# An attention and mixture-of-experts kernel: rows of q and k and gathered rows transposed as f32r instead of f32

## The chip, the cores and the metric

The kernel runs on 1 core of one Trainium2 chip. A core has five engines that run side by side, each with its own queue: PE (TensorE, matrix products into PSUM), DVE (VectorE), ACT (ScalarE), POOL (GpSimd) and SP (SyncE, which here only issues DMAs). PEld is the part of PE that loads the stationary operand. All DMAs of a core share 16 DMA engines. The metric is the device time of one execution in microseconds, lower is better. Before the change three runs took 766.83, 770.14 and 770.59 us (median 770.14).

## What is computed

First an attention with a hash mask: batch 4, 8 heads, 768 positions, head dimension 64. A query sees only keys whose six sign bits (of x times a random projection) agree with its own.

```python
q_bits = (np.einsum('bhsd,dk->bhsk', q, proj) > 0)
k_bits = (np.einsum('bhsd,dk->bhsk', k, proj) > 0)
mask = q_bucket[:, :, :, None] == k_bucket[:, :, None, :]   # buckets are the bits read as a number
scores = np.where(mask, scale * q @ k^T, -1e9)
attn = softmax(scores)
x = (attn @ v) as [3072 tokens, 512]
```

Then one expert of eight for each token, of sizes 512 to 1024 to 512:

```python
logits = x @ w_gate + modality_bias[modality_id]
e_idx = np.argmax(logits, axis=1); gate_w = softmax(logits) at e_idx
out[tokens of e] = gate_w * (relu(x @ w1[e]) @ w2[e])
```

All inputs and outputs are float32.

## The kernel before

**Numbers as two parts.** A float32 matrix product is made of f32r products, a form of float32 that PE takes in one pass: an operand is split into a rounded part and a residue (`m1` and `s2`, `xh` and `xl`, `hi` and `lo`), and two or three products are summed in PSUM. Which form PE uses is set by the type of the tiles.

**Attention.** The work goes by pairs of heads, 16 pairs, numbered i (0 to 15). The loop over i runs `score(i)` (scores and exponentials), `maxp(i + 1)` (the maxima that the softmax subtracts), `turn(i + 2)` and `signs(i + 2)` (rows of q and k transposed, hash bits), `residues(i + 2)` (the rounded parts and residues, and DMAs from SBUF to SBUF that spread them over the other 64 partitions), `weigh` (the product with v) and some pieces of the row sums and the router. The order on PE is written out by hand: `PLAN0` for i = 0, `PLAN` for 1 to 14, `LAST` for 15, one string for each of six steps `kt`, one letter for a piece. `T` is one group of four transposes of `turn` (three groups to a pair) or the hash bits, `R` the residues, `L` the load of pair i + 3, `l` the load of v. The other engines and SP's DMAs are put in order by a scheduler, which follows this order and what is ready; SP works its queue strictly in order.

**Rows of q and k.** `load(i)` (L117) issues four DMAs on SP, one each for q and k of each head of the pair, into a tile `qk` of which there are two (pool `ld`). Each has 768 pieces of 256 bytes, since q and k lie side by side in the tile. `turn(i)` (L288) transposes four blocks of 128x128 into a PSUM tile `psx` (L299), the moving operand being the unit matrix `ident` (f32), and ACT copies the tile back over the same place of `qk` (L300), the "raw rows", which the hash bits (L218) and the residues (L307, L308) read. Pair 1 has a form of its own, `second` (L252), and pair 0 too (L184).

**Experts.** Tokens are gathered by slots of 512 rows: `gather` (L925) fetches rows of x from DRAM by an indirect DMA of POOL into `xg`, `xprep` (L941) transposes them, four 128x128 blocks for each `psx` tile (L956), ACT and DVE split them into `xh` and `xl`, and `gemm1` (L967) and `gemm2` (L1008) multiply. Six slots of 512 rows and one of 128 (L949) are always run.

**Two unit matrices.** `ident` is f32, `identr` its copy in f32r, made by POOL (L159). `identr` is used for the transposes of the maxima (L368), whose input `nm` or `nw` is an f32r tile.

Of the kernel before, what the change touches and what calls it, by code (L numbers as in the profile page):

```python
# [10 lines left out]
F32 = mybir.dt.float32  # L11
# [9 lines left out]
NT = S // 128  # L21
# [15 lines left out]
    "SRMSeMSMx",  # L37
    "SFfEMSfMSMF",
    "fSMSMMEBABSe",
# [5 lines left out]
    "MSMlSMRM",  # L45
    "SMSMML",
    "MMBASB",
# [45 lines left out]
def attention(ctx, actx, tc, a, x_d, l_d, route=None, setup=None, before_last=None):  # L93
# [20 lines left out]

    st, fin = {}, {}

    def load(i, heads=(0, 1), parts=1):  # L117
        b, c = i // 4, i % 4
        t = st.setdefault(i, {})
        if "qk" not in t:  # L120
            t["qk"] = ld.tile([P, 2, NT, 2, D], F32, name="qk")
        n = NT // parts
        for h in heads:
            qk = t["qk"][:, h]
            for lo in range(0, NT, n):
                for x, src in enumerate((q, k)):
                    nc.sync.dma_start(out=qk[:, lo:lo + n, (x + 1 + h) % 2], in_=src[b, 2 * c + h].rearrange("(p t) d -> p t d", t=NT)[:, lo:lo + n])
# [10 lines left out]
    nc.scalar.dma_start(out=zst[64:128, 6:12], in_=proj)  # L138
    load(0, (0,), 2)
    ident = fconst.tile([P, P], F32, name="ident")  # L140
    nc.scalar.dma_start(out=ident, in_=a["c_id"])
# [8 lines left out]
    fold = fconst.tile([P, TT], F32, name="fold")  # L150
    identr = const.tile([P, P], F32R, name="identr")
    masks = [const.tile([P, S], F32, name=f"mask{j}") for j in range(2)]
# [99 lines left out]
    def second():  # L252

        t = st[1]
        t.update(gens[0])
        rows = t["qk"].rearrange("p h t x d -> p (h t x d)")
        raw = t["raw"] = [rows[:, h * S:(h + 1) * S] for h in range(2)]
# [30 lines left out]
    def turn(i):  # L288

        t = st[i]  # L290
        t.update(gens[(i + 2) % 3])
        rows = t["qk"].rearrange("p h t x d -> p (h t x d)")
        raw = t["raw"] = [rows[:, h * S:(h + 1) * S] for h in range(2)]
        todo = [(h, tt) for h in range(2) for tt in range(NT)]
        for g in range(0, len(todo), 4):
            part = todo[g:g + 4]
            tp = ps_x.tile([P, MAIN], F32, name="psx")
            for j, (h, tt) in enumerate(part):
                nc.tensor.transpose(tp[:, j * P:(j + 1) * P], t["qk"][:, h, tt].rearrange("p x d -> p (x d)"), ident)  # L299
            nc.scalar.copy(out=rows[:, g * P:(g + 4) * P], in_=tp)  # L300
            yield
# [278 lines left out]
    with tc.manual_schedule(engines={mybir.EngineType.PE}):  # L580
        load(1)
        load_v(0)
        load(2)
        constants()
        with tc.manual_schedule(engines={mybir.EngineType.DVE, mybir.EngineType.Activation, mybir.EngineType.Pool}):
# [16 lines left out]
        for i in range(NPR):  # L602
# [8 lines left out]
            for kt in range(NT):  # L611
# [5 lines left out]
                for c in (PLAN0 if i == 0 else LAST if i == NPR - 1 else PLAN)[kt]:  # L617
# [20 lines left out]
                    elif c == "L":  # L638
                        if i + 3 < NPR:
                            load(i + 3)  # L640
                    elif c == "l":
                        if i + 1 < NPR:
                            load_v(i + 1)
                    elif c == "F" and i % 4 == 0 or c == "f" and i % 4 == 1:
                        next(fins, None)
                    elif c == "e" and i % 4 >= 2 or c == "E" and i == NPR - 2:
                        next(fins, None)
                    elif c == "x" and i % 4 == 2 or c == "y" and i % 4 == 3:
                        next(xs, None)
                        next(xs, None)  # L650
        for _ in avs:
            pass
    return finish, finish_x, ps_x, ident, fold, marks

# [219 lines left out]

def experts(ctx, tc, a, x_d, tab, out, ps_x, ident, fold, marks):
    nc = tc.nc
    w1, w2 = a["moe_w1"], a["moe_w2"]
    gp = ctx.enter_context(tc.tile_pool(name="gp", bufs=1))
# [46 lines left out]
    def gather(s):  # L925
# [4 lines left out]
        nc.sync.dma_start(out=tb[:, 0:n], in_=tab[bass.ds(o, n * P), :].rearrange("(p a) w -> p a w", a=n))  # L930
        xg = gp.tile([P, TS // P, DM], F32, name="xg", bufs=XG)
        src, at = x_d, tb[:, :, 0:1]
# [4 lines left out]
        for g in range(n):  # L937
            nc.gpsimd.indirect_dma_start(out=xg[:, g], out_offset=None, in_=src, in_offset=bass.IndirectOffsetOnAxis(ap=at[:, g], axis=0))  # L938
        return tb, xg

    def xprep(s, xg, dst):  # L941
# [4 lines left out]
        if nt(s) == 1:  # L946
            tp = ps_x.tile([P, 4, P], F32, name="psx")
            for c in range(4):
                nc.tensor.transpose(tp[:, c], xg[:, 0, c * P:(c + 1) * P], ident)  # L949
            nc.scalar.copy(out=xh[:, :, 0:P], in_=tp)  # L950
            nc.vector.tensor_tensor(out=xl[:, :, 0:P], in0=tp, in1=xh[:, :, 0:P].bitcast(F32), op=ALU.subtract)
            return
        for c in range(4):
            tp = ps_x.tile([P, TS], F32, name="psx")
            for g in range(nt(s)):
                tr = nc.tensor.transpose(tp[:, g * P:(g + 1) * P], xg[:, g, c * P:(c + 1) * P], ident)  # L956
                if s == ("e", 0):
# [227 lines left out]
def body(tc, a, out):  # L1185
# [4 lines left out]
    with ExitStack() as ctx, ExitStack() as actx:  # L1190
        route, early_slots, late_slots, setup = router(ctx, tc, a, x_d, tab)
        finish, finish_x, ps_x, ident, fold, marks = attention(ctx, actx, tc, a, x_d, None, route, setup, lambda sp: eslot.append(early_slots(sp)))
        actx.close()
        runner, tabs, conditional, yp, late_area, tiny = experts(ctx, tc, a, x_d, tab, out, ps_x, ident, fold, marks)
        r = runner()
# [38 lines left out]
```

## Time and profile before

| | |
|---|---|
| runs, us | 766.83, 770.14, 770.59 |
| profiled execution, us | 766.3 |
| its span (first to last instruction), us | 764.4 |
| PE busy | 744.9 us, 97% |
| DVE, ACT, POOL busy | 65%, 48%, 57% |
| DMA of SP's queue | 83.79 MB, 44.4% of the 16 engines |

How to read it: PE is busy nearly all the time, but a matrix product is pipelined, and its "busy" time holds its latency, so that the share alone does not say whether PE could do more. What PE's work costs in time is read from the starts of consecutive instructions. The span has four parts: a start of about two passes, up to 58 us; the attention's steady loop, up to 444 us; the expert slots, up to about 710 us; and an end.

### The profile page before, as it was taken

How to read it: one execution, taken by the hardware profiler on the slowest of the kernel's cores; microseconds unless marked ns; L12 is line 12 of the kernel's file. 1: busy time of each engine (PE TensorE's matmuls, PEld its weight loads, DVE VectorE, ACT ScalarE, POOL GpSimd, SP SyncE). 2: the span in 40 equal slices, each digit the busy share in tenths (PEclk: the TensorE clock that was granted, in tenths of full speed). 3: DMA queues.
4: the chain of work that ended last, by engine and by line, in shares of the span. 5: the costliest groups of instructions: out<-in, count | busy, mean ns of one | idle time of the engine just before them, and what ended most of it. 6: DMA issues, size and time to landing. Idle time of an engine off the chain costs nothing.

```text
span 764.4 us, 12253 instructions
## 1 busy us (share of the span) xinstructions
PE 744.9 (97%) x4308; PEld 527.8 (69%) x4308; DVE 499.3 (65%) x878; ACT 367.2 (48%) x649; POOL 438.6 (57%) x335
## 2 busy tenths in 40 slices
PE   7899999999999999999999999999999999999995
PEld 3566666566656666666666657888888877788884
DVE  6987778788777887976986887844333343334423
ACT  5455565555555556556564563244243432434343
POOL 7697779769878868987869974622222202202011
PEclk9999999999999999999999999999999999999998
DMA  8655454526766435665343154665444754444332
GB/s 191 141 127 126 91 123 114 130 67 120 130 132 140 112 85 125 134 120 141 91 101 60 56 194 129 112 216 179 139 156 134 254 196 138 143 123 137 103 109 74
DMA packets 103528, 99.26 MB, mean 130 GB/s; under 512 B 60333, under 2 KB 80717, under 8 KB 103456
## 3 DMA queue, kind: packets, MB, share of 16 engines
q1 hardware_dynamic: 97312, 83.79, 44.4%
q0 software_dynamic: 4832, 12.94, 4.8%
q10 hardware_dynamic: 1312, 1.65, 1.1%
q8 instruction: 36, 0.59, 0.3%
q14 instruction: 36, 0.29, 0.2%
HBM read 59.33 MB, written 13.14 MB: 95 GB/s over the span
## 4 chain that ended last, share of the span: by engine, by line
PE 83%; issue 9%; DVE 3%; DMA 1%; POOL 1%; ACT 1%; SPq 0%; POOLq 0%; DVEq 0%; ACTq 0%
PE psu L457 16%; PE pss L404 9%; PE pss L405 8%; PE psm L339 6%; PE hps L974 5%; PE hps L975 5%; PE hps L976 5%; PE yps L1017 4%; PE yps L1015 4%; PE yps L1016 4%; PE psm L345 3%; PE psx L299 2%; PE psu L218 2%; PE psx L480 2%; PE psx L542 1%
## 5 line engine op out<-in xcount | busy, mean ns | idle before, releaser
L441 POOL TENSOR_TENSOR sp<-sp,pb 128x768 f32<-128x768 f32 x124 | 225.8, 1855 | 14.1 <-ACT pb L438 13.2
L341 DVE TENSOR_REDUCE mx<-psm 128x1 f32<-128x512 f32 x192 | 130.1, 687 | 26.4 <-PE psm L339 24.1
L424 ACT ACTIVATE pb<-pss 128x512 f32<-128x512 f32 x186 | 111.3, 599 | 60.2 <-PE pss L405 51.6
L457 PE MATMUL psu<-pb,vt 128*64 128x512 f32 (+1 forms) x768 | 134.4, 492 | 0.0
L922 DVE TENSOR_TENSOR w<-raw,w 128x1024 fp32r<-128x1024 f32 x52 | 65.6, 1264 | 100.7 <-ACT w L918 100.2
L457 PEld LDWEIGHTS psu<-pb,vt 128*64 128x64 f32 x768 | 50.9, 136 | 69.9 <-issue 60.0
L918 ACT CAST w<-raw 128x1024 fp32r<-128x1024 f32 x56 | 58.5, 1049 | 79.1 <-PE yps L1017 72.2
L438 ACT ACTIVATE pb<-pss 128x512 f32<-128x512 f32 x93 | 55.6, 598 | 81.2 <-PE pss L405 79.4
L1084 POOL DMA_INDIRECT out<-y,tb x25 | 24.8, 990 | 106.5 <-ACT y L1083 102.9
L441 POOL TENSOR_TENSOR sp<-pb,pb 128x768 f32<-128x768 f32 x31 | 56.2, 1836 | 50.0 <-ACT pb L438 50.0
L1015 PE MATMUL yps<-w,hl 128*128 128x512 f32 x200 | 79.5, 397 | 0.0
L1017 PE MATMUL yps<-w,hh 128*128 128x512 f32 x200 | 78.2, 391 | 0.0
L1016 PE MATMUL yps<-w,hh 128*128 128x512 f32 x200 | 77.9, 389 | 0.0
L974 PE MATMUL hps<-xh,w 128*128 128x512 f32 x192 | 75.4, 394 | 0.0
L938 POOL DMA_INDIRECT xg<-x_d,tb x17 | 18.2, 1069 | 98.8 <-DMA tb<-tab 95.2
L975 PE MATMUL hps<-xl,w 128*128 128x512 f32 x192 | 74.9, 390 | 0.0
L976 PE MATMUL hps<-xh,w 128*128 128x512 f32 x192 | 74.7, 390 | 0.0
L404 PE MATMUL pss<-m_0g,s_0g 128*128 128x512 f32 (+1 forms) x186 | 69.5, 374 | 0.4
L979 ACT ACTIVATE hh<-hps 128x512 fp32r<-128x512 f32 x48 | 28.7, 598 | 83.4 <-PE hps L976 83.4
L980 DVE SCALAR_TENSOR_TENSOR hl<-hps,hh 128x512 fp32r<-128x512 f32 x48 | 33.2, 691 | 53.7 <-ACT hh L979 53.4
L347 DVE TENSOR_REDUCE mx<-psm 128x2 f32<-128x512 f32 x96 | 66.1, 688 | 1.2
L404 PE MATMUL pss<-m_1g,s_1g 128*128 128x512 f32 (+1 forms) x186 | 65.9, 355 | 0.1
(266 smaller groups left out, 1428.4 us busy)
## 6 DMA issues: line engine op xcount, KB each, us to landing
raw<-moe_w SPq DMA_DIRECT2D x56, 512.0 KB
vt<-v SPq DMA_DIRECT2D x16, 384.0 KB
qk<-q SPq DMA_DIRECT2D x31, 192.0 KB
qk<-k SPq DMA_DIRECT2D x31, 192.0 KB
s_0g<-m_0g SPq DMA_DIRECT2D x30, 192.0 KB
s_1g<-m_1g SPq DMA_DIRECT2D x30, 192.0 KB
x_d<-xs SPq DMA_DIRECT2D x18, 256.0 KB
tw<-moe_w SPq DMA_DIRECT2D x2, 2048.0 KB
```

Source lines behind the costliest of these rows:

```text
L341: marks["m"] = nc.vector.tensor_reduce(out=mx[:, qt + j, hi, 0:1], in_=mp, axis=AX.X, op=ALU.max).ins
L347: nc.vector.tensor_reduce(out=mx[:, qt:qt + 2, hi, 1], in_=mp, axis=AX.X, op=ALU.max)
L404: nc.tensor.matmul(out, t["s1"][h][:, ks], t["m1"][h][:, cs], start=True, stop=False)
L424: marks["p"] = nc.scalar.activation(t["pb"][kt][:, h, 0:MAIN], sp, AF.Exp, scale=0.125).ins
L441: marks["add"] = (nc.vector if h and i in CFG["spd"] else nc.gpsimd).tensor_tensor(out=t["sp"][:, h], in0=(t["pb"][0] if kt == 1 else t["s ...
L457: marks["u", kt] = nc.tensor.matmul(t["u"][part][64 * h:64 * h + 64, 0:w], t["v"][:, h, kt], t["pb"][kt][:, h, COLS[part]], start=False, s ...
L974: nc.tensor.matmul(hps, lo[:, c, fs], xh[:, c], start=(c == 0), stop=False)
L975: nc.tensor.matmul(hps, hi[:, c, fs], xl[:, c], start=False, stop=False)
L976: nc.tensor.matmul(hps, hi[:, c, fs], xh[:, c], start=False, stop=(c == 3))
L1015: nc.tensor.matmul(yps[g], hl[fc][:, gs], hi[:, fb], start=(fc == 0), stop=False)
L1016: nc.tensor.matmul(yps[g], hh[fc][:, gs], lo[:, fb], start=False, stop=False)
L1017: nc.tensor.matmul(yps[g], hh[fc][:, gs], hi[:, fb], start=False, stop=(fc == 7))
```

## The change

Pairs 3 to 15 of q and k no longer go to SBUF directly. A new `stage(i)` copies them by four DMAs from DRAM to a scratch tile in DRAM that has the layout of `qk`, and `load(i)` fetches that with one DMA into an f32r tile. `stage(3)` stands after `load(2)` ahead of the loop, and a new letter `c` in step 4 of the plans stages pair i + 4. For these pairs `turn` transposes as f32r with `identr`. The raw rows get a tile of their own: in `turn` the other one of the two `qk` tiles, in `second` one of the two `sp` tiles. The gathered rows `xg` are an f32r tile too, written by the indirect DMA under the name of f32, and transposed as f32r. `identr` moves to another pool, and the experts use it in place of `ident` (as f32 where they need that).

```diff
-    "SFfEMSfMSMF",
+    "ScFfEMSfMSMF",
...
-    "SMSMML",
+    "SMSMMLc",
...
+    scratch = {}
+
+    def stage(i):
+
+        b, c = i // 4, i % 4
+        scratch[i] = tc.dram_tile([P, 2, NT, 2, D], F32, name=f"qk_d{i}")
+        for h in range(2):
+            for x, src in enumerate((q, k)):
+                nc.sync.dma_start(out=scratch[i][:, h, :, (x + 1 + h) % 2], in_=src[b, 2 * c + h].rearrange("(p t) d -> p t d", t=NT))
 
     def load(i, heads=(0, 1), parts=1):
         b, c = i // 4, i % 4
         t = st.setdefault(i, {})
+        if i in scratch:
+            t["qk"] = ld.tile([P, 2, NT, 2, D], F32R, name="qk")
+            nc.sync.dma_start(out=t["qk"].bitcast(F32), in_=scratch[i])
+            return
...
+    identr = fconst.tile([P, P], F32R, name="identr")
     ident = fconst.tile([P, P], F32, name="ident")
...
-    identr = const.tile([P, P], F32R, name="identr")
...
@@ second
-        rows = t["qk"].rearrange("p h t x d -> p (h t x d)")
+        rows = spool.tile([P, 2, S], F32, name="sp").rearrange("p h s -> p (h s)")
...
@@ turn
-        rows = t["qk"].rearrange("p h t x d -> p (h t x d)")
+        rows = ld.tile([P, 2, S], F32, name="qk").rearrange("p h s -> p (h s)")
...
-                nc.tensor.transpose(tp[:, j * P:(j + 1) * P], t["qk"][:, h, tt].rearrange("p x d -> p (x d)"), ident)
+                nc.tensor.transpose((tp.bitcast(F32R) if i in scratch else tp)[:, j * P:(j + 1) * P], t["qk"][:, h, tt].rearrange("p x d -> p (x d)"), identr if i in scratch else ident)
...
         load(2)
+        stage(3)
...
+                    elif c == "c":
+                        if i + 4 < NPR:
+                            stage(i + 4)
...
-        xg = gp.tile([P, TS // P, DM], F32, name="xg", bufs=XG)
+        xg = gp.tile([P, TS // P, DM], F32R, name="xg", bufs=XG)
...
-            nc.gpsimd.indirect_dma_start(out=xg[:, g], out_offset=None, in_=src, in_offset=bass.IndirectOffsetOnAxis(ap=at[:, g], axis=0))
+            nc.gpsimd.indirect_dma_start(out=xg[:, g].bitcast(F32), out_offset=None, in_=src, in_offset=bass.IndirectOffsetOnAxis(ap=at[:, g], axis=0))
...
-                tr = nc.tensor.transpose(tp[:, g * P:(g + 1) * P], xg[:, g, c * P:(c + 1) * P], ident)
+                tr = nc.tensor.transpose(tp.bitcast(F32R)[:, g * P:(g + 1) * P], xg[:, g, c * P:(c + 1) * P], identr)
```

The order of instructions on the engines shows what the scheduler makes of it. First PE in the second pass of the loop, where pair 3 is turned, before (L299 is the transposes, L404 and L405 the scores of pair 1, L339 and L345 the maxima of pair 2):

```order
L339 MATMUL psm<-s_0g_115,m_0g_113 128x512
L404 MATMUL pss<-m_0g_102,s_0g_104 128x512
L405 MATMUL pss<-m_0g_106,s_0g_108 128x512
L299 MATMUL psx<-ident,qk 128x128 x4
L404 MATMUL pss<-m_1g_103,s_1g_105 128x512
L405 MATMUL pss<-m_1g_107,s_1g_109 128x512
L299 MATMUL psx<-ident,qk 128x128 x4
L339 MATMUL psm<-s_0g_115,m_0g_113 128x512
```

And PE at the same place now (the lines have new numbers: L312 is the transposes, L417, L418, L352 are L404, L405, L339 of before):

```order
L352 MATMUL psm<-s_0g_115,m_0g_113 128x512
L417 MATMUL pss<-m_0g_102,s_0g_104 128x512
L418 MATMUL pss<-m_0g_106,s_0g_108 128x512
L312 MATMUL psx<-identr,qk 128x128 x4
L417 MATMUL pss<-m_1g_103,s_1g_105 128x512
L418 MATMUL pss<-m_1g_107,s_1g_109 128x512
L312 MATMUL psx<-identr,qk 128x128 x4
L352 MATMUL psm<-s_0g_115,m_0g_113 128x512
```

Nothing moved on PE; `identr` stands for `ident`, in 39 groups of four.

Next SP at the start, before, from the load of v on (L206 and L207 spread the residues of pair 0, the four L127 load pair 2, the rest are small constants):

```order
L133 DMA vt<-v 128x2x384
L206 DMA m_0g_128<-m_0g_124 64x768
L207 DMA s_0g_130<-s_0g_126 64x768
L588 DMA wg<-moe_w_gate 128x4x8
L706 DMA ktok<-c_tok 128x24
L706 DMA ke_66<-c_e 128x24
L127 DMA qk<-q 128x6x64
L127 DMA qk<-k 128x6x64
L127 DMA qk<-q 128x6x64
L127 DMA qk<-k 128x6x64
L206 DMA m_1g_129<-m_1g_125 64x768
L207 DMA s_1g_131<-s_1g_127 64x768
```

SP at the start now (L124 is the copies to the scratch, L140 the loads, L219 and L220 are L206 and L207 of before):

```order
L146 DMA vt<-v 128x2x384
L124 DMA qk_d_204<-q 128x6x64
L124 DMA qk_d_204<-k 128x6x64
L124 DMA qk_d_204<-q 128x6x64
L124 DMA qk_d_204<-k 128x6x64
L140 DMA qk<-q 128x6x64
L140 DMA qk<-k 128x6x64
L140 DMA qk<-q 128x6x64
L140 DMA qk<-k 128x6x64
L219 DMA m_0g_128<-m_0g_124 64x768
L220 DMA s_0g_130<-s_0g_126 64x768
L219 DMA m_1g_129<-m_1g_125 64x768
```

The copies for pair 3 and the loads of pair 2 moved ahead of the spread of head 0 of pair 0, and the small constants went further back, behind the mask rows of pair 1 (L246).

Last SP in the steady loop, before, between two pairs' spreads (L312 spreads mask rows, L318 begins the next pair's residues):

```order
L312 DMA m_1g_114<-mask_175 12x384 x2
L127 DMA qk<-q 128x6x64
L127 DMA qk<-k 128x6x64
L127 DMA qk<-q 128x6x64
L127 DMA qk<-k 128x6x64
L133 DMA vt<-v 128x2x384
L312 DMA s_0g_126<-mask_176 12x384 x2
L312 DMA s_1g_127<-mask_176 12x384
L318 DMA m_0g_128<-m_0g_124 64x768
```

And SP at the same place now (L131 is the load from the scratch):

```order
L325 DMA m_1g_114<-mask_175 12x384 x2
L124 DMA qk_d_745<-q 128x6x64
L124 DMA qk_d_745<-k 128x6x64
L124 DMA qk_d_745<-q 128x6x64
L124 DMA qk_d_745<-k 128x6x64
L124 DMA qk_d_1000<-q 128x6x64
L124 DMA qk_d_1000<-k 128x6x64
L131 DMA qk<-qk_d_745 128x1536
L146 DMA vt<-v 128x2x384
L124 DMA qk_d_1000<-q 128x6x64
L325 DMA s_1g_127<-mask_176 12x384 x2
L331 DMA m_0g_128<-m_0g_124 64x768
```

Between two pairs' spreads there are now six or seven copies, one load and the load of v, where four loads and the load of v stood. A copy waits for nothing, so the scheduler puts it earlier than the letter `c` says: the last of the 52 copies stands some five passes ahead of pair 15's turn.

## Rows read from the trace of the kernel before

**Rows 1.** Windows: stretch, length, busy us of PE, PEld, DVE, ACT, POOL, clock, DMA share, GB/s
```profile
0.00:30.00 30.00, 22.40 (x112) 11.59 (x112) 23.39 (x42) 13.79 (x27) 23.29 (x48) 0.94 0.78 169
58.00:444.00 386.00, 384.77 (x2510) 248.78 (x2510) 308.12 (x572) 214.98 (x411) 313.33 (x203) 1.00 0.49 109
470.00:710.00 240.00, 240.00 (x1151) 196.06 (x1150) 103.82 (x176) 88.31 (x128) 55.60 (x52) 1.00 0.52 159
710.00:764.40 54.40, 45.70 (x229) 38.17 (x227) 19.05 (x21) 20.07 (x30) 4.90 (x5) 0.95 0.31 94
```
**Rows 2.** Groups of PE instructions by form: line, tiles, shapes, count, busy us, mean ns
```profile
L299 PE MATMUL psx<-ident,qk 128*128 128x128 f32 x168 | 25.1, 272 | 0.0
...
L956 PE MATMUL psx<-ident,xg 128*128 128x128 f32 x96 | 13.5, 276 | 1.3 <-DVE xl L963 0.7 <-DMA xg<-x_d,at 0.6
L368 PE MATMUL psx<-identr,nm 128*128 128x128 f32 x90 | 12.2, 245 | 0.0
```
**Rows 3.** Timeline of PE around one group of L299: start us, us, what
```profile
36.28 0.60 PE L299 MATMUL psx<-ident,qk 128*128 128x128 f32 x4
36.64 0.48 PE L404 MATMUL pss<-m_1g,s_1g 128*128 128x512 f32 x1
36.95 0.39 PE L405 MATMUL pss<-m_1g,s_1g 128*128 128x512 f32 x1
```
**Rows 4.** Timeline of PE around one group of L368, f32r
```profile
29.93 0.43 PE L368 MATMUL psx<-identr,nw 128*128 128x128 f32 x4
30.20 0.47 PE L404 MATMUL pss<-m_0g,s_0g 128*128 128x512 f32 x1
30.50 0.40 PE L405 MATMUL pss<-m_0g,s_0g 128*128 128x512 f32 x1
```
**Rows 5.** Timeline of PE around one group of eight of L956
```profile
505.18 1.03 PE L956 MATMUL psx<-ident,xg 128*128 128x128 f32 x8
505.97 0.47 PE L1015 MATMUL yps<-w,hl 128*128 128x512 f32 x1
506.28 0.39 PE L1016 MATMUL yps<-w,hh 128*128 128x512 f32 x1
506.51 0.40 PE L1017 MATMUL yps<-w,hh 128*128 128x512 f32 x1
```
**Rows 6.** Timeline of PE in the first slot's transposes
```profile
453.26 0.33 PE L956 MATMUL psx<-ident,xg 128*128 128x128 f32 x1 [0.31 <-DMA xg<-x_d,at]
...
458.10 1.25 PE L956 MATMUL psx<-ident,xg 128*128 128x128 f32 x8 [0.71 <-DVE xl L963]
```
**Rows 7.** Waits of PEld from 58 to 444 us: total us, times, longest
```profile
PEld pss L404 <- ACT pb L438: 10.8, 25, 0.8
...
PEld pss L404 <- ACT pb L424: 4.3, 13, 0.4
```
**Rows 8.** DMA queue of SP from 294 to 301 us: packets, MB, share
```profile
q1 hardware_dynamic: 2449, 0.64, 49.7%
```
**Rows 9.** DMA queue of SP from 150 to 370 us
```profile
q1 hardware_dynamic: 35608, 26.23, 55.8%
```
**Rows 10.** Timeline of SP's DMA issues at the start
```profile
8.48 0.54 SPq L206 DMA_DIRECT2D m_0g<-m_0g  x1
...
13.98 0.73 SPq L127 DMA_DIRECT2D qk<-k  x1
14.81 1.11 SPq L206 DMA_DIRECT2D m_1g<-m_1g  x1
```
**Rows 11.** Timeline of PE: the first product that reads a spread residue of pair 0
```profile
23.13 0.40 PE L405 MATMUL pss<-m_0g,s_0g 128*128 128x512 f32 x1
```
**Rows 12.** Timeline of SP's DMA issues in the steady loop
```profile
277.49 0.39 SPq L133 DMA_DIRECT2D vt<-v  x1
281.08 1.63 SPq L312 DMA_DIRECT2D s_0g<-mask  x2
...
294.68 0.61 SPq L127 DMA_DIRECT2D qk<-q  x1
```

More of the change, by code (lines that the diff above doesn't have):

```diff
@@ L652, in attention @@
             pass
-    return finish, finish_x, ps_x, ident, fold, marks
+    return finish, finish_x, ps_x, identr, fold, marks
 N = B * S
@@ L872, in router, with experts @@
     return route, early_slots, late_slots, setup
-def experts(ctx, tc, a, x_d, tab, out, ps_x, ident, fold, marks):
+def experts(ctx, tc, a, x_d, tab, out, ps_x, identr, fold, marks):
     nc = tc.nc
+    ident = identr.bitcast(F32)
     w1, w2 = a["moe_w1"], a["moe_w2"]
@@ L948, in xprep @@
             for c in range(4):
-                nc.tensor.transpose(tp[:, c], xg[:, 0, c * P:(c + 1) * P], ident)
+                nc.tensor.transpose(tp.bitcast(F32R)[:, c], xg[:, 0, c * P:(c + 1) * P], identr)
             nc.scalar.copy(out=xh[:, :, 0:P], in_=tp)
@@ L1191, in body @@
         route, early_slots, late_slots, setup = router(ctx, tc, a, x_d, tab)
-        finish, finish_x, ps_x, ident, fold, marks = attention(ctx, actx, tc, a, x_d, None, route, setup, lambda sp: eslot.append(early_slots(sp)))
+        finish, finish_x, ps_x, identr, fold, marks = attention(ctx, actx, tc, a, x_d, None, route, setup, lambda sp: eslot.append(early_slots(sp)))
         actx.close()
-        runner, tabs, conditional, yp, late_area, tiny = experts(ctx, tc, a, x_d, tab, out, ps_x, ident, fold, marks)
+        runner, tabs, conditional, yp, late_area, tiny = experts(ctx, tc, a, x_d, tab, out, ps_x, identr, fold, marks)
         r = runner()
```

## The prediction

> **What bounds the kernel now.** I read the windows first, then the groups of PE's instructions, then the timeline around single groups, and last the DMA queue. The windows [rows 1] show PE busy for 384.77 of 386 us in the steady loop and for all 240 us of the expert slots, at full clock, while DVE, ACT and POOL have room (308, 215 and 313 of 386 us). A busy PE need not be a PE without slack, so the starts decide: in the expert slots the 512-column products follow each other every 0.23 us, and the one after a group of transposes 0.31 us later, with no idle time shown [rows 5]. Work taken from PE in these two parts should come off the time. The start is different: PE is busy 22.4 of 30 us there and DVE 23.4, while the DMA engines run at 0.78. The end (710 on) waits for other things and is left alone.
>
> **The change part by part.**
>
> *Transposes as f32r.* What one costs is seen from the starts, since its own duration (272 ns as f32, 245 as f32r [rows 2]) overlaps the next. Four f32 transposes and the product behind them take from 36.28 to 36.95, so 0.67 us up to the second product [rows 3]. The same with four f32r ones takes from 29.93 to 30.50, 0.57 us [rows 4]. Part of the gain is given back: the four f32r ones are through after 0.27 us instead of 0.36, and the product behind them starts its successor 0.30 later, as after f32. Gain per group of four: 0.10 us.
>
> *How many.* 168 transposes in L299 [rows 2] are 42 groups; pair 2's three groups stay f32, as the order on PE shows, which leaves 39. 39 x 0.10 = 3.9 us. Of L956's 96 [rows 2], most stand in groups of eight, 12 in all. Eight f32 take 0.79 us up to the next product and 1.10 to the second one [rows 5]. With two times 0.27 for eight f32r [rows 4] and the same 0.30 behind, it is 0.84, a gain of 0.26; twice a group of four would be 0.20. I take 0.22. Two of the twelve stand in the first slot, where PE waits for the gather's DMA and for DVE between its transposes [rows 6]: there a shorter transpose only waits longer, 0. So 10 x 0.22 = 2.2 us. The four of the small slot gain 0.1, which I leave out. Together 6.1 us.
>
> *What is swallowed.* In the steady loop the scores wait for ACT to free their bank, 38 times, 15.1 us in total, 0.4 us each [rows 7]; that is two or three times in a pass, while three groups a pass are made shorter. A group whose gain falls into such a wait gives nothing. From below: all three do, the gain of 3.9 is gone; from above: none. The waits are short and follow the two products of a bank, not the transposes, so I take a quarter as lost, 1.0 us. In the experts nothing like this shows.
>
> By the Trainium skill, "TensorE: Matmul & The Clock Gate", section "LDWEIGHTS (loading the stationary operand)", a load of 128 columns takes 107 ns by the formula given there; since every transpose loads its own block, four could not follow each other faster than 0.43 us and f32r would gain nothing. The f32r group took 0.27 us for four, 68 ns each [rows 4], so the trace does not agree with it; by the rule the sum would lose all 6.1 us.
>
> *The raw rows.* ACT's three copies of a pair write another tile, of the same shape. The tile's earlier reader (hash bits and residues of the pair before) is done a pass earlier by the order, so no wait is added. The load of pair i + 3 now goes to the tile that `turn(i + 2)` has just transposed, so SP waits for the third group. Behind it on SP stands the load of v, which waits for PE anyway (277.49 in [rows 12], with SP free before it), and then mask rows, which need the hash bits that PE makes after that group. The load is used a pass later. Cost 0; if that cover failed, the mask rows at 281.08 would be late by what SP waits beyond 281.
>
> *The copies in the steady loop.* A load of 3072 pieces of 256 bytes per pair becomes 3072 copied pieces, plus a load of 128 pieces of 6144 bytes. From 294 to 301 us the queue moved almost only such pieces: 49.7% of 16 engines in 7 us are 55.7 us for 2449 packets, 22.7 ns each [rows 8]. No row shows a copy from DRAM to DRAM. From below: it costs what the load cost, 3072 x 22.7 / 16 = 4.4 us of all engines for a pair (even less in total is possible, as the load itself now has few large pieces; that moves nothing, since no engine waits for it). From above I take the mean over all packets in the loop, large ones and those that cross SBUF twice: 55.8% of 16 x 220 us over 35608 packets = 55 ns [rows 9], 10.6 us a pair. Six or seven copies of 768 pieces a pass make this 6.5 to 18 us. The engines are idle for half of a pass of 27.6 us (386 us hold 14 passes; share 0.49 [rows 1]), some 14 us, so at the lower end it fits beside the rest. SP has the time to issue: it idles from the last load (294.68 and three more) to the next load of v, about a pass after 277.49 [rows 12]. I take 0, nearest to the row that moves the same pieces.
>
> *The copies at the start.* Here the engines are full. Before, the spread of head 0 of pair 0 was issued at 8.48, ahead of pair 2's loads [rows 10]; now four copies and those four loads go first, and it is issued at about 14, where the loads ended before (13.98 + 0.73). Its pieces are first read by the product at 23.13 [rows 11]. In the queue ahead of it stand the loads of three pairs (9216 pieces, 13.1 us at 22.7 ns), v (0.39 MB at 169 GB/s [rows 1], 2.3 us) and the copies (4.4 us): 19.8 us of engine time, begun about 2 us after the first instruction, so about 22, and the spread itself about 1 us more. That is at 23, just where it is needed. With copies at 55 ns it is 29, 6 us late. From below it is 0 or a gain of a microsecond, since the small constants that stood ahead of pair 1's spreads now follow them. I take a loss of 1.0 us, near the lower end, where the row with the same pieces lies.
>
> *The rest* (`identr` in another pool, `sp` for the raw rows of pair 1, POOL's small copies later among the adds): POOL's adds of pair 0 stood behind the constants before as well; 0, at most some tenths.
>
> **Sum.** -6.1 + 1.0 + 1.0 = -4.1 us. The profiled execution took 766.3 us (span 764.4), so it would take 762.2. It lies 3.8 us below the median of the three runs, 770.14; from the median the forecast is 766.
>
> **Rivals.**
>
> *The gain is lost in waits.* The waits for ACT [rows 7] take all of 3.9, the start costs 2 instead of 1, and the experts' 2.2 remain: 770.1 - 2.2 + 2 = 770. For it: 38 waits against 39 groups. Against it: most of the steady products follow each other without a wait.
>
> *The transposes are no shorter.* Another input than that of L368, or the weight load as the limit: 0 gained, 1 lost at the start, 771. Against it: the same form of instruction, 128x128 with `identr`, stands in [rows 4]. The only doubt is that those groups read one column spread over 128, while these read 128 different ones.
>
> *The copies fill the queue (slower).* Six or seven copies stand directly ahead of the next pair's mask rows and residues, and the engines work a queue in order. Six copies are 288 pieces for each engine; the removed load (4.4 us) and the new one (0.79 MB, 4.3 us at the rate of [rows 8]) cancel. So the idle 14 us of a pass are full when a copied piece costs 49 ns, and from there each further 10 ns makes a pass 2.9 us longer, because PE waits for m1 and s1 of the next pair at its head. At 55 ns it is 1.8 us over, in the eight passes that carry copies 14 us, and the start costs 6: 770.1 - 6.1 + 20 = 784. For it: small pieces, both sides in DRAM, and a share of 0.78 at the start. Against it: 22.7 ns for the same pieces into SBUF. By the Trainium skill, "DMA: Bandwidth & Descriptors", section "Specifications", a transfer below 512 bytes makes the DMA engine read, modify and write. I estimate from that a doubled piece, 45 ns, just short of the point; no run here shows it, and by it the start would cost 4.4 us more, and the time be 770.
>
> **Chances.** Forecast 0.53, with a range of its own of 762 to 769; gain lost in waits 0.28; no shorter transposes 0.06; queue filled 0.13. A difference under 0.5% (3.9 us) is about what these runs can't tell from no change, as they spread by 3.8 us themselves. The forecast lies at that edge, with its larger part beyond it, and the start may also cost nothing, so of its 0.53 I count 0.46 as faster, and 0.05 of the second case; slower is the filled queue: faster 0.51, same 0.36, slower 0.13. Range 761 to 773: the lower end is the whole 6.1 and 3 us of the runs' spread, the upper end the second rival's 770 and the same 3 us; the queue filled beyond its point lies outside.
>
> **What the profile after would show.** Each step can be seen: groups of four in the turns with 0.57 us to the second product; groups of eight with 0.84 to 0.90; PE's busy time lower by some 6 us or more with the other engines' unchanged; the first product on pair 0's residue at 23 to 24 us; the passes shorter by 0.2 to 0.3 us each; q1's share up by some points with about 1700 packets more. The prediction is wrong if the f32r transposes still start 109 ns apart, if waits for ACT grow by what the transposes lose, or if PE shows waits for DMAs in the first 60 us or at the heads of the passes.

## The result and the profile after

The changed kernel took 773.81 us (median of 15 runs), the kernel before 767.2 us in the same rounds: ratio 1.0073, 95% interval 1.0051 to 1.0095. It is slower, by 5.6 us by the ratio (6.6 by the medians); forecast were 4.1 us less, and the range ended at 773. The profiled execution took 771.9 us, its span is 770.1 (before: 766.3 and 764.4).

The windows of the changed kernel (columns as in [rows 1]), beside those of before [rows 1]:

```profile
0.00:30.00 30.00, 22.64 (x111) 11.28 (x112) 21.39 (x42) 13.80 (x27) 22.15 (x42) 0.94 0.86 189
58.00:444.00 386.00, 382.51 (x2500) 247.31 (x2500) 303.83 (x562) 214.89 (x410) 311.15 (x202) 0.99 0.56 134
470.00:710.00 240.00, 240.00 (x1171) 194.65 (x1170) 106.41 (x187) 88.36 (x128) 56.56 (x53) 1.00 0.52 161
710.00:770.10 60.10, 51.97 (x257) 43.40 (x255) 21.65 (x24) 22.22 (x33) 4.90 (x5) 0.97 0.34 103
```

The instruction counts tell more than the busy times: up to 444 us PE got through fewer instructions than before (2500 for 2510 in the loop), though its transposes are shorter. By the starts of the same instruction in the two traces, PE is 6.2 us behind at 440 us, 7.9 at 470 and 6.4 at 693: the loss lies ahead of the slots, and the slots give 1.5 us back. The waits of PE up to 450 us show where (total us, times, longest):

```profile
PE psm L352 <- DMA s_0g<-mask: 7.3, 4, 3.5
PE psm L358 <- DVE mx L354: 2.0, 4, 0.8
```

The first row has no counterpart before. The longest of these waits is in the first pass. PE there (start us, duration, instruction, idle time before it):

```profile
53.02 0.28 PE L418 MATMUL pss<-m_1g,s_1g 128*128 128x256 f32 x1
53.14 0.28 PE L381 MATMUL psx<-identr,nm 128*128 128x128 f32 x2
56.91 0.77 PE L352 MATMUL psm<-s_0g,m_0g 128*128 128x512 f32 x1 [3.48 <-DMA s_0g<-mask]
57.47 0.63 PE L417 MATMUL pss<-m_0g,s_0g 128*128 128x512 f32 x1
57.90 0.63 PE L418 MATMUL pss<-m_0g,s_0g 128*128 128x512 f32 x1
```

L352 (L339 of before) reads the mask rows of `s1` of head 0, and they have not landed. Behind the wait the 512-column products take 0.63 us, where they took 0.39 before [rows 3]. The windows around it show why: the granted clock is 0.50, the lower of the two levels.

```profile
47.00:53.00 6.00, 5.71 (x35) 3.16 (x34) 5.35 (x11) 2.02 (x4) 5.84 (x7) 1.00 0.61 152
53.00:57.00 4.00, 0.52 (x6) 0.41 (x4) 1.26 (x3) 0.60 (x1) 4.00 (x4) 0.89 0.12 29
57.00:63.00 6.00, 6.00 (x23) 4.91 (x24) 2.07 (x3) 2.74 (x5) 3.56 (x2) 0.50 0.74 168
63.00:69.00 6.00, 6.00 (x50) 3.19 (x48) 2.08 (x6) 3.41 (x8) 0.49 (x1) 1.00 0.74 220
```

The same products in the trace of before, and the second of them in the trace after:

```profile
52.79 0.46 PE L339 MATMUL psm<-s_0g,m_0g 128*128 128x512 f32 x1
56.08 0.40 PE L405 MATMUL pss<-m_0g,s_0g 128*128 128x512 f32 x1
```
```profile
62.50 0.61 PE L418 MATMUL pss<-m_0g,s_0g 128*128 128x512 f32 x1
```

The product that began at 52.79 begins at 56.91, 4.1 us later, and the one of 56.08 at 62.50, 6.4 later. Of the 4.1 us, 0.5 had been lost before the wait (the product of 52.08 began at 52.56). SP tells why the rows were late (its DMA issues, start and duration):

```profile
40.61 0.74 SPq L325 DMA_DIRECT2D s_0g<-mask  x1
41.45 0.75 SPq L325 DMA_DIRECT2D s_1g<-mask  x1
42.30 0.52 SPq L331 DMA_DIRECT2D m_0g<-m_0g  x1
...
45.73 1.02 SPq L331 DMA_DIRECT2D m_1g<-m_1g  x1
49.48 0.47 SPq L333 DMA_DIRECT2D s_0g<-m_0g  x1
...
52.29 1.60 SPq L325 DMA_DIRECT2D m_0g<-mask  x2
53.94 0.71 SPq L325 DMA_DIRECT2D s_1g<-mask  x1
54.70 0.71 SPq L325 DMA_DIRECT2D s_0g<-mask  x1
```

Before, both halves of `s_0g`'s mask rows stood at the head of the pass; here is the trace of before at the same place:

```profile
40.27 1.63 SPq L312 DMA_DIRECT2D s_0g<-mask  x2
```

Now one half follows only behind the residue spreads (L330 to L333, which wait for each other's landing from 46.75 to 49.48) and the other mask rows: issued at 54.70 instead of 41.1, used 2.2 us later. The scheduler had put one or both halves there in the other passes too; at 218.72 it is both, and PE waits 2.00 us at 221.60.

What the change was meant to shorten did get shorter. A group of eight in the experts after, and one of four in the turns (of the kernel with the order mended, e_order below, where the clock is full):

```profile
512.94 0.80 PE L974 MATMUL psx<-identr,xg 128*128 128x128 f32 x8
513.57 0.47 PE L1033 MATMUL yps<-w,hl 128*128 128x512 f32 x1
513.88 0.40 PE L1034 MATMUL yps<-w,hh 128*128 128x512 f32 x1
```
```profile
55.53 0.46 PE L312 MATMUL psx<-identr,qk 128*128 128x128 f32 x4
55.83 0.47 PE L421 MATMUL pss<-m_1g,s_1g 128*128 128x512 f32 x1
56.13 0.39 PE L422 MATMUL pss<-m_1g,s_1g 128*128 128x512 f32 x1
```

Eight take 0.63 us and 0.94 up to the second product, where it was 0.79 and 1.10 [rows 5]; four take 0.30 and 0.60, where it was 0.36 and 0.67 [rows 3].

### The profile page after: what moved, and what is told of

Read it like the earlier page. It is cut to its first block, busy times and chain, and to the rows that moved or that the text cites. A ratio compares the mean times of both kernels' runs of the same rounds, so it can differ in the third digit from the quotient of the medians.

```text
span 770.1 us, 12212 instructions
## 1 busy us (share of the span) xinstructions
PE 744.5 (97%) x4308; PEld 525.3 (68%) x4308; DVE 496.2 (64%) x878; ACT 367.0 (48%) x649; POOL 437.6 (57%) x335
## 4 chain that ended last, share of the span: by engine, by line
PE 79%; issue 9%; DMA 5%; DVE 3%; ACT 1%; SPq 1%; POOL 1%; POOLq 0%; DVEq 0%; ACTq 0%
PE psu L470 15%; PE pss L417 9%; PE pss L418 8%; PE psm L352 6%; PE hps L992 5%; PE hps L994 5%; PE hps L993 5%; PE yps L1033 4%; PE yps L1035 4%; PE yps L1034 4%; PE psm L358 3%; PE psu L231 2%; PE psx L312 2%; PE psx L493 2%; DMA m_0g<-s_0g 1%
## 5 line engine op out<-in xcount | busy, mean ns | idle before, releaser
L470 PE MATMUL psu<-pb,vt 128*64 128x512 f32 (+1 forms) x768 | 136.1, 497 | 0.0
L956 POOL DMA_INDIRECT xg<-x_d,tb x17 | 17.8, 1046 | 99.3 <-DMA tb<-tab 86.7
L417 PE MATMUL pss<-m_0g,s_0g 128*128 128x512 f32 (+1 forms) x186 | 70.2, 378 | 0.4
L417 PE MATMUL pss<-m_1g,s_1g 128*128 128x512 f32 (+1 forms) x186 | 66.0, 355 | 0.0
```

What stands on the lines that cost most here:

```text
L417: nc.tensor.matmul(out, t["s1"][h][:, ks], t["m1"][h][:, cs], start=True, stop=False)
L470: marks["u", kt] = nc.tensor.matmul(t["u"][part][64 * h:64 * h + 64, 0:w], t["v"][:, h, kt], t["pb"][kt][:, h, COLS[part]], start=False, s ...
```

## The experiments

Theory A: the loss is SP's order, the late mask rows. Rival B: the copies, by what they take of the DMA queue. Rival C: shorter transposes give nothing, they only lengthen other waits. Ratios are to the kernel before in the same rounds, with the 95% interval.

**e_order**: the two mask rows get a high priority, all else in the code is the changed kernel (on SP the scheduler then also moves some copies and loads).

```diff
-        for (dst, _), src in t["places"]:
-            nc.sync.dma_start(out=dst.bitcast(F32), in_=src)
+        for j, ((dst, _), src) in enumerate(t["places"]):
+            if j in (4, 5):
+                with tc.high_priority(offset=1000):
+                    nc.sync.dma_start(out=dst.bitcast(F32), in_=src)
+            else:
+                nc.sync.dma_start(out=dst.bitcast(F32), in_=src)
```

> The changed kernel, with one thing altered: in every pass SP issues the two mask rows of s1 of head 0 (s_0g<-mask) ahead of the residue spreads again, as the kernel before does; copies, scratch and f32r transposes all stay. Theory A (the late mask rows are what was lost): no wait of PE for s_0g<-mask, the clock stays up at 58 us, the 4.1 us of idle and the 2 us of half clock at the start of the loop and the 2 us at 221 us are gone. What is left is 2.8 us gained in the turns and 2 in the experts against 0.3 to 1 us at the start: ratio to before 0.993 to 0.996, about 763 to 765 us beside 767. Rival B (the copies take room in the queue, or SP is held at the load from the scratch, and the late rows only show it): another DMA wait takes the place of this one, ratio 1.003 to 1.009.

Measured: 0.9983 (0.996 to 1.0006), 770.27 us beside 771.13. The wait is gone and the clock stays up; the same product as above:

```profile
54.17 0.29 PE L385 MATMUL psx<-identr,nm 128*128 128x128 f32 x2
54.76 0.47 PE L356 MATMUL psm<-s_0g,m_0g 128*128 128x512 f32 x1 [0.30 <-issue]
```

Some 7 us came back (1.0073 to 0.9983 of 767; 5.6 by e_order2 below), as A says, but hardly any gain over before is left, which A had not expected.

**e_late**: the kernel before, with these rows made late by an order without a wait.

```diff
+        ins = []
         for (dst, _), src in t["places"]:
-            nc.sync.dma_start(out=dst.bitcast(F32), in_=src)
+            ins.append(nc.sync.dma_start(out=dst.bitcast(F32), in_=src).ins)
+        for j in (4, 5):
+            behind(ins[j], ins[3], "the mask rows of s1 of head 0 come after those of m1 of head 0 and s1 of head 1")
```

> The kernel before, with one thing altered: the mask rows of s1 of head 0 are issued behind those of m1 of head 0 and s1 of head 1, and so behind the residue spreads, in every pass. No copies, no scratch, f32 transposes. Theory A: PE waits for s_0g<-mask at the first pass for 3 to 4 us, the clock falls behind that wait, and two or three later passes wait 1 to 2 us: slower by 6 to 9 us, ratio 1.008 to 1.012. Rival B (it needs the copies in the queue or the load from the scratch on SP): no wait above 0.5 us, ratio 1.000 to 1.002.

Measured: 1.006 (1.0036 to 1.0083), 775.36 us. The wait is there without a copy, though shorter (total, times, longest):

```profile
PE psm L342 <- DMA s_0g<-mask: 2.8, 3, 1.6
```

The order alone makes the kernel 4.6 us slower, a little less than expected. The waits explain 2.8 of it, and by the starts PE is 3.1 us behind before at 440 us; what the rest is, one trace does not show. The wait in the first pass was 0.24 us (at 54.83) and not 3 to 4, so the expected size per pass was wrong.

**e_xg**: the experts' part alone (`xg` as f32r and `identr` there, the rest as before).

```diff
-        xg = gp.tile([P, TS // P, DM], F32, name="xg", bufs=XG)
+        xg = gp.tile([P, TS // P, DM], F32R, name="xg", bufs=XG)
...
-                tr = nc.tensor.transpose(tp[:, g * P:(g + 1) * P], xg[:, g, c * P:(c + 1) * P], ident)
+                tr = nc.tensor.transpose(tp.bitcast(F32R)[:, g * P:(g + 1) * P], xg[:, g, c * P:(c + 1) * P], identr)
```

> The kernel before, with the experts' part of the change alone: gathered rows land in f32r tiles and are transposed as f32r; rows of q and k stay as they were. By the starts of the groups of eight in the two traces (889 ns before, 722 after) ten groups should give 1.7 us, and the stretch from 462 to 693 us gave 2 us: ratio 0.997 to 0.998, about 1.7 to 2 us less, all of it behind 470 us. The rival that shorter transposes only lengthen other waits expects no difference, ratio 0.999 to 1.001.

Measured: 0.9993 (0.9976 to 1.0009). By the runs inconclusive: the interval holds 0.998 and 1. Its trace is 4.7 us behind before at 498 us, nearly all of it lost in the first expert slot; e_again tells what that is. From 499 to 693 us it gains 1.5 us, and so does every trace whose gathered rows are f32r, while e_again and e_late, which transpose them as f32, gain 0.0 there. So in the slots the shorter transposes do come off the time.

**e_order_f32t**: as e_order, the turns' transposes f32 again.

```diff
-                nc.tensor.transpose((tp.bitcast(F32R) if i in scratch else tp)[:, j * P:(j + 1) * P], t["qk"][:, h, tt].rearrange("p x d -> p (x d)"), identr if i in scratch else ident)
+                nc.tensor.transpose(tp[:, j * P:(j + 1) * P], t["qk"].bitcast(F32)[:, h, tt].rearrange("p x d -> p (x d)"), ident)
```

> As e_order (scratch, copies, raw rows in their own buffer, mask rows of s1 of head 0 first), but the turns' transposes of q and k read the same tiles as f32; the experts' stay f32r. Against the kernel before it adds the copies and the move on SP, without what they were for. Theory A: the copies cost only what they cost at the start, 0.3 to 1 us, and the experts give 2: ratio 0.998 to 1.000, and 2.8 us more than e_order, a ratio to it of 1.003 to 1.004. Rival B (copies in the queue cost by themselves): 1.005 or more. Rival C (f32r transposes in the turns gain nothing): the same time as e_order.

Measured: 1.0002 (0.9981 to 1.0024). That is where A put it, but too near to e_order to part A from C. In its profiled execution PE waits 3.7 us for `m_0g<-mask` at 219 us: SP issues those mask rows at 217.14 there, at 209.44 before. The profile puts 2.6 us of SP's waits there down to the landing of a copy (`qk_d<-k`). So the copies can matter in that pass; in e_order, with the same copies, the rows are issued at 209.44 and PE does not wait.

**e_twice**: as e_order, each copy made twice.

```diff
+        twice = tc.dram_tile([P, 2, NT, 2, D], F32, name=f"tw_d{i}")
...
                 nc.sync.dma_start(out=scratch[i][:, h, :, (x + 1 + h) % 2], in_=src[b, 2 * c + h].rearrange("(p t) d -> p t d", t=NT))
+                nc.sync.dma_start(out=twice[:, h, :, (x + 1 + h) % 2], in_=src[b, 2 * c + h].rearrange("(p t) d -> p t d", t=NT))
```

> As e_order, but every copy of a pair's rows into a scratch is issued twice, the second time to a scratch that nobody reads: 52 more DMAs, 39936 more pieces of 256 bytes. It is the dose that tells what the copies cost in the queue. If copies in the queue cost little (13 pairs, the engines half idle), the start loses about 3 us more, since the copies of pair 3 stand there twice, and the passes nothing: ratio to before 1.001 to 1.004. Rival B (the copies crowd the queue in the passes that carry them): waits of PE for DMAs at the heads of several passes, each with a fall of the clock behind it, 10 us or more: ratio above 1.012.

Measured: 1.0363 (1.0328 to 1.0399), 801.67 us: B. The queue's line of the page of e_order (packets, MB, share of 16 engines), then of e_twice:

```profile
q1 hardware_dynamic: 99184, 94.01, 47.2%
```
```profile
q1 hardware_dynamic: 139952, 104.24, 50.6%
```

50.6% of 16 x 803.1 us less 47.2% of 16 x 764.0 are 732 us for 39936 copied pieces, 18.3 ns each: cheap, and the share rises by three points only. Yet it is some 29 us slower than e_order by the ratios (1.0363 and 0.9983). SP's waits show how, in e_order first and then in e_twice:

```profile
SPq L337 <- DMA m_0g<-s_0g: 21.3, 14, 2.9
```
```profile
SPq L339 <- DMA m_0g<-s_0g: 49.2, 14, 7.7
```

The second spread waits for the landing of the first, which has the copies ahead of it. But the order changed too: in seven passes the load from the scratch stands directly ahead of the spreads (at 178.44, the first spread at 179.67), where in e_order it is issued some us earlier, ahead of the mask rows of `s_0g` (191.00 and 201.13). So e_twice is not the dose alone, and how its loss divides between the two is not shown. The mask rows stand behind all that, and PE in e_twice waits for them:

```profile
PE psm L358 <- DMA m_0g<-mask: 15.3, 4, 4.5
```

**e_again and e_after2**: the kernel before and the changed kernel once more, one profile each.

> The kernel before once more, nothing changed. Its trace tells whether the waits in the first expert slot (480 to 500 us: PE for DVE's hl, xl or tslot, with half a clock behind one of them), which are 2 to 5 us longer in the traces of e_xg, e_late and e_order than in that of before, belong to these kernels or differ from one execution to the next. If they belong to the kernels, this trace shows no wait above 0.7 us there, as before; if they differ by execution, it may show waits of 1 to 2 us, and a span some us away from 764.4.

Measured: 770.37 us, span 768.4. From 470 to 505 us PE waited for nothing in the first trace of before; in this one:

```profile
PE yps L1015 <- DVE tslot L821: 1.3, 1, 1.3
PE hps L974 <- DVE hl L980: 0.8, 1, 0.8
PE psx L542 <- DVE over L862: 0.7, 1, 0.7
```

The same kernel is 4.5 us later at 500 us. These waits differ by execution; the trace that I predicted from was one of the good ones, and e_xg's loss there says nothing on e_xg.

> The changed kernel once more, unchanged. Theory A (its loss belongs to SP's order, which is fixed when it is built): the wait of PE for s_0g<-mask at the first pass behind 50 us, 3 to 4 us with the clock's fall behind it, stands in this execution too. If that wait was chance of one execution, as those of the first expert slot are, it is absent or below 1 us.

Measured: 778.91 us. The wait of the first pass is there again: PE stands 4.2 us behind before at that product (4.1 in the first trace), and 6.5 at the one of 56.08 (6.4). It belongs to the kernel.

**e_nostage3**: as e_order, without `stage(3)`, so that pair 3 is loaded directly.

> As e_order (mask rows of s1 of head 0 first in every pass), and pair 3 is no longer copied at the start: its rows are loaded straight from q and k and transposed as f32, so that SP's order in the first 20 us is that of before. Theory A (the start costs what the copies and the residue spreads behind them take): e_order's trace is 1.7 us behind that of before at 20 us; this goes, while 3 groups of four lose 0.07 us each: 1.5 us less than e_order, ratio to before 0.995 to 0.997. Rival (the start is not set by SP's order there): PE stands at 20 us where it stands in e_order, ratio as that of e_order, 0.998.

Measured: 1.0016 (0.9985 to 1.0048). At 20 us PE is 0.9 us ahead of before, as A said, but so it is in e_again, where nothing was changed; this says nothing on the start. And the load of pair 3 now comes behind the first copies of pair 4:

```profile
PE psx L312 <- DMA qk<-k: 3.8, 1, 3.8
```

A miss by my own edit: the wait moved, it did not go.

**e_start**: as e_order, `stage(3)` behind the opening of pair 0.

```diff
-        stage(3)
         constants()
         with tc.manual_schedule(engines={mybir.EngineType.DVE, mybir.EngineType.Activation, mybir.EngineType.Pool}):
             opening = first()
+        stage(3)
```

> As e_order, with the call that copies pair 3's rows moved behind the opening of pair 0, so that SP issues the residue spreads of head 0 of pair 0 ahead of the copies and of pair 2's loads, as before. Theory A (the copies at the start push the spreads back): the 1.7 us that e_order has lost by 20 us in its trace go, pair 3's copies still land well before they are loaded; ratio to e_order 0.998, to before 0.995 to 0.997. Rival (the copies cost what they take of the queue, wherever in the first 50 us they stand): no gain against e_order, 0.998 to before, with a new wait of PE for a DMA between 30 and 58 us.

Measured: 0.999 (0.9964 to 1.0016). A falls for the start: its trace is 2.7 us late at 13 us as e_order's is, while e_order2, which has e_order's order, is not. So the start differs by execution too, and its SP order is not what sets it.

**e_order2**: e_order once more.

> e_order once more, unchanged, since its first interval (0.996 to 1.0006) leaves open whether anything is gained. By the gains of the groups in the traces (2 to 3 us in the turns, 1.7 in the experts, 1.7 lost at the start) the ratio to before is 0.996 to 0.998. If the copies take the rest of the gain in the passes: 0.999 to 1.002.

Measured: 1.0 (0.9972 to 1.0027). With the mask rows in place the changed kernel is as fast as before, and no more. Where the copies stand, SP's own issue is held up in some executions. The mask rows at the head of the pass near 225 us, each time two DMAs, before, in e_order, in e_start and in e_pace:

```profile
224.57 1.62 SPq L312 DMA_DIRECT2D s_0g<-mask  x2
```
```profile
225.28 5.01 SPq L327 DMA_DIRECT2D s_0g<-mask  x2
```
```profile
227.43 5.45 SPq L327 DMA_DIRECT2D s_0g<-mask  x2
```
```profile
225.61 1.63 SPq L329 DMA_DIRECT2D s_0g<-mask  x2
```

In the changed kernel it is a copy that takes 4.63 us to issue, at 200.74. In both traces of before no single issue between 58 and 444 us takes above 1.8 us. What the held-up issue costs PE is not shown. From 210 to 260 us PE falls back against before by 0.3 us in e_order, 3.1 in e_order2, 5.5 in e_start and 7.1 in e_order_f32t, and gains 0.4 in e_nostage3; e_again (0.9 gained) and e_xg (0.1 gained), which have no copies, do not fall back there. So this stretch takes gain away in most kernels with copies, and not by the same amount in two executions of one kernel.

**e_pace**: as e_order, and a pair's copies stand behind the mask rows of their pass, four a pass over twelve passes. **e_pace_f32t**: the same with the turns' transposes f32.

```diff
-                nc.sync.dma_start(out=scratch[i][:, h, :, (x + 1 + h) % 2], in_=src[b, 2 * c + h].rearrange("(p t) d -> p t d", t=NT))
+                cp = nc.sync.dma_start(out=scratch[i][:, h, :, (x + 1 + h) % 2], in_=src[b, 2 * c + h].rearrange("(p t) d -> p t d", t=NT))
+                if "masks" in marks:
+                    behind(cp.ins, marks["masks"], "a pair's copies come after the mask rows of its pass")
...
-                nc.sync.dma_start(out=dst.bitcast(F32), in_=src)
+                marks["masks"] = nc.sync.dma_start(out=dst.bitcast(F32), in_=src).ins
```

> As e_order, and the copies of a pair are held behind the mask rows of the pass in which they are called, so that SP issues four copies a pass over twelve passes, where e_order issues six or seven a pass and is through with them by 250 us. Theory (with the mask rows in place, what still eats the gain is the DMA queue in the passes from 190 to 260 us, where copies, x_d's stores, the load and v come together and PE waits at the head of a pass): no wait of PE for a DMA above 1 us between 190 and 260 us, PE there 1 to 2 us ahead of e_again instead of level with it or behind, ratio to before 0.994 to 0.997. Rival (the gain never was in the time: shorter transposes only lengthen the waits for ACT and DVE): ratio 0.999 to 1.001 as e_order2.

Measured: 0.9978 (0.996 to 0.9995), 768.79 us beside 770.23. It beats before by 1.7 us, if barely, and, by the ratios, the changed kernel by about 7, but e_order's first ratio was 0.9983: that pacing the copies helps is not shown. It stays short of what was expected: no wait for a DMA between 190 and 260 us, but one that ends at 244.69 us and for which the profile names nothing. PE is behind e_again there, not ahead, and falls back by 3.1 us from 210 to 260 us, with four copies a pass:

```profile
PE psm L358 <- issue: 2.8, 1, 2.8
```

Before this product SP issues the mask rows of `m_0g`, which it reads, before and in e_pace:

```profile
237.32 1.74 SPq L312 DMA_DIRECT2D m_0g<-mask  x2
```
```profile
241.42 1.60 SPq L331 DMA_DIRECT2D m_0g<-mask  x2
```

They are 4.1 us later; SP had waited 4.0 us for the landing of a spread up to 237.33. PE goes on 2.4 us after the second half is issued, and 2.4 us after it too in e_start, where it waits 3.64 us for "issue" in the same pass. This points to late mask rows once more; the profile does not show it.

> As e_pace, with the turns' transposes of q and k as f32 again (the experts' stay f32r). Both theories take the same copies and the same order here, so the difference is what f32r gives in the turns: by the groups in the traces 39 times 0.071 us = 2.8 us, e_pace over this 0.996 to 0.997. If shorter transposes only lengthen other waits: 1.000 to each other.

Measured: 1.0007 (0.9991 to 1.0023). e_pace over this is 0.9978 / 1.0007 = 0.997, 2.2 us (from the single runs of both, 95% interval about 0.9 to 3.4), which agrees with the 2.8 expected from the groups: C falls for the turns.

## Why the prediction was wrong

**The step that failed** is that the mask rows keep their place on SP at no cost. It stands in "The raw rows", in its words "Cost 0; if that cover failed, the mask rows at 281.08 would be late by what SP waits beyond 281", and "The copies in the steady loop" takes 0 as well, from engine time and SP's idle time, without asking what the copies do to SP's order. I asked when SP would be free for these rows and took their place in the queue from the trace of before [rows 12]. That place had changed: the piece of SP's order with the copies, ahead of the prediction, has `s_1g_127<-mask` and the spread `m_0g_128<-m_0g_124` next, and `s_0g_126<-mask` is gone from between. The row was in sight and was read for the copies alone.

The trace after shows which part of the change goes with it. At the head of every pass from 42 to 235 us at least one half of `s_0g`'s mask rows stands behind the residue spreads. The last copy is issued at 230; in the six passes from 262 us on both halves stand ahead again, although the load from the scratch, the raw rows' own tile and the f32r transposes are there as well. The pass of [rows 12] is one of these:

```profile
288.32 1.53 SPq L325 DMA_DIRECT2D s_0g<-mask  x2
```

That is 7.2 us after 281.08, as far as PE is behind there. So the cover that I priced held in the pass that I read it from, and the rows lost their place where the copies stand. Why the scheduler moves them there is not shown.

The lost place costs 5.6 to 6.9 us (1.0073 against 1.0 and 0.9983); another late order without any copy costs 4.6 us (e_late). At the first wait PE falls back by 3.6 us through the wait and by 2.3 through the lower clock behind it, and the forecast had no term for either.

**The copies in the steady loop**: the price of a piece was near the lower end (18.3 ns; 22.7 was taken), and the cost of 0 was still wrong. With the order mended, the kernels with copies keep little of what the transposes gain (0.9983, 1.0; paced 0.9978), and the loss between 210 and 260 us comes with four copies a pass as with six or seven. Twice the number, in another order, costs 29 us. The rival "the copies fill the queue" had the right wait and the wrong condition: it counted free engine time over a pass and found the point at 49 ns a piece. The spreads are a chain of landings with SP waiting in between, and in e_twice this chain delays the mask rows at a share of 50.6%, long before the engines are full. By the Trainium skill, "DMA: Bandwidth & Descriptors", section "Specifications", transfers below 512 bytes make the engine read, modify and write; the estimate of 45 ns from it does not agree with the 18.3 ns.

**Transposes as f32r**: right in kind, a third too large. A group of four gives 0.07 us, not 0.10, one of eight 0.16, not 0.22: 39 x 0.07 + 10 x 0.16 = 4.3 us, not 6.1. I had taken 0.27 us for four from [rows 4], and these take 0.30. That is 75 ns each, so the weight-load time of 107 ns in the Trainium skill, "TensorE: Matmul & The Clock Gate", section "LDWEIGHTS (loading the stationary operand)", does not bound them; that rival was wrong.

**What is swallowed**: waits for ACT did not grow; the two rows that answer to [rows 7] are

```profile
PEld pss L417 <- ACT pb L451: 10.8, 25, 0.8
...
PEld pss L417 <- ACT pb L437: 4.1, 12, 0.4
```

and the quarter that I left out is not seen. By the starts, the 15 groups between 60 and 210 us bring PE forward by 1.0 us in the traces of after, e_order, e_order2 and e_pace (0.0 in e_again); 15 times 0.071 is 1.07. The runs of e_pace and e_pace_f32t, 2.2 of 2.8 us, do not tell a quarter from nothing.

**The copies at the start**: the spread was issued at 15.62 instead of 8.48, and the first product on the residue began at 23.18 (23.13 before [rows 11]): covered. The traces differ by up to 2.7 us there between executions of one kernel, so the 1.0 us can't be told from 0.

**Still open**: what ends the wait near 245 us in e_pace, what makes the stretch from 210 to 260 us so different between executions with copies, and whether pacing helps. The experts' share of the gain, 1.6 us by the groups and 1.5 by the starts, is not told from 0 by the runs of e_xg.

## What to carry to other kernels

When a change adds instructions to a queue that a scheduler orders, read the new order of that queue whole, and ask of each instruction that PE waits for where it stands now; the place of before proves nothing. A transfer that nobody waits for can still cost, where it changes the order of a queue or stands ahead of a chain of short ones; pacing it alone did not bring the gain back here. And one trace is one execution: a second one of the same kernel showed which gaps are its own.

## What was unexpected in the hardware

SP's issue of one DMA, 0.6 to 0.8 us elsewhere, took 4.2 to 6.1 us once in each of five executions with six or seven copies in most passes, though the DMA share of the loop was only 0.55 to 0.57; e_nostage3 and e_order_f32t, with as many copies, had none above 2.6. A wait of PE of 3.48 us was followed by some 6 us at half clock, one of 2.00 us (at 221.60) by none. The longest wait alone does not decide: in the first expert slot of the same trace, waits of 0.15, 0.72 and 0.17 us between single transposes (459.9 to 461.3) were followed by a clock of 0.50 at 463 to 465 us. Executions of the kernel before lay between 765.4 and 777.7 us over all rounds; the traces show the start (up to 2.7 us) and the first expert slot (4.5 us) as places where executions of one kernel part.
